# phi(K) as one maximum on VectorE, with new instruction orders, in a linear-attention and gated-GELU block on one core

## The chip, the core and the metric

The kernel runs on one NeuronCore of one Trainium2 chip. Its metric is device time in microseconds, the median of several runs. The engines are named as the profile names them: PE (TensorE), DVE (VectorE), ACT (ScalarE), POOL (GpSimd) and SP (SyncE, which here only issues DMAs).

## The reference

One sequence of 2048 tokens with 448 features goes through a pre-norm linear attention (16 heads of 28) and a gated-GELU feed-forward layer of width 1792, each with a residual. All inputs are bf16.

```python
qkv = (layernorm(x) @ wqkv)                     # split into q, k, v per head
phi = lambda t: jnp.where(t > 0, t + 1, jnp.exp(t)) + 1e-6
pq, pk = phi(q), phi(k)
kv = einsum("bhsd,bhse->bhde", pk, v)
z = einsum("bhsd->bhd", pk)
num = einsum("bhqd,bhde->bhqe", pq, kv)
den = einsum("bhqd,bhd->bhq", pq, z)[..., None] + 1e-6
h = x + merge_heads(num / den) @ wo
g, u = layernorm(h) @ w_gate, layernorm(h) @ w_up
out = h + (gelu_tanh(g) * u) @ w_down
```

## The kernel before

Tokens are cut into 16 tiles of 128 (T = 16); a pair is two tiles. The kernel is a graph of small named tasks. Each belongs to one engine, and every engine works through its tasks in an order written out as numbers in `ORDERS` (lines 15 to 49; one string each for PE, ACT, DVE, POOL and SP). The function `place` (line 129) takes those orders; the waits between engines are semaphores worked out from what each task reads and writes. So an order says only when an engine comes to a task; a task still waits for its inputs and for the buffer that it overwrites. `HOLD` (line 50) names, for some tasks that wait for two others, which of the two waits is written first.

Stage 1 (to about 34 us). For each tile: statistics (`bnst1_t`, `bnag1_t`, lines 413 and 414, DVE), the reciprocal root in two activations (`ln1_t`, `rstd1_t`, lines 420 and 422, ACT), normalisation and transpose. Tiles 0 to 3 are normalised on DVE (`normD_t`, line 435) and transposed on PE in two halves (`tr0_t`, `tr1_t`, line 443), copied out by ACT (`evxA_t`) and DVE (`evxD_t`, line 450). Tiles 4 to 15 are normalised on POOL (`normP_t`, line 453) and transposed by a DMA that SP issues (`xT_t`, line 455).

Then come the projections, four matmuls each: `k_t` and `q_t` (`proj`, line 469), in the sequence that PE's order gives. They take their PSUM banks in turn from four (`slot`), in the sequence of `SEQ`, so that each waits until the one four places earlier has been read. The contraction is over 448 rows in four chunks of 128; the last chunk has 64 rows of weights, and its other 64 rows of `wqk_sb` are set to zero (`wqkpad`, line 364). In the transposed input the rows that meet them hold ones, for the columns 448 to 511 of `xnn` are set to 1 (`ones2`, line 386).

phi(K) is made from the projected tile in PSUM, psK, in three steps: ACT writes exp(K) to `e1` (`ek_t`, line 480); DVE clamps it to at most 1 + 1e-6 (`ck_t`, line 481); DVE adds to it the larger of K and 1e-6 (`pk_t`, line 482). The sums over tokens are kept as four accumulating groups of matmuls over all 16 tiles, in PSUM banks 4 to 7: each tile gives four matmuls (line 488, `pt4_t`; from tile 10 on split as `pt1_t`, chunk 3, and `pt3_t`, chunks 0 to 2), with the normalised input `xnn` as weights and `pk` as the moving operand. The ones in `xnn` make the lower half of chunk 3 the sum z.

From the sums to the attention output (about 32 to 50 us): z is copied to both halves of `zbc` (`z1` on ACT, `z0` on DVE, lines 514 and 515), the four sums go to `pt_sb` (`evpD_3` and `evpD_2` on DVE, `evpA_0` and `evpA_1` on ACT, lines 516 to 521), `kv` multiplies them by the value weights (line 527), `kvm` (line 531) masks out other heads, `w2_c` multiplies by wo (line 547). For the first pair, `cq`, `aq`, `t1`, `dr`, `deA`, `rd` and `pn` (lines 564 to 576) make phi(Q) divided by its denominator. PE fills the waits with the projections `q_4` to `q_15`, then transposes the first pair of normalised h (`trh`, line 654).

Stage 2 (about 50 us to the end): for every chunk of tiles `gu` (lines 731 and 733) makes gate and up projections in two PSUM banks each, ACT applies the GELU (`ge`, line 751), DVE multiplies (`hm`, line 753); the down projections (`down`, lines 678 and 697), the final additions (`fo`) and the stores (`do_t`) follow. The attention outputs of later pairs (`outA`, `outB`, lines 627 and 628) are placed between them.

Of the kernel before, what the change touches and what calls it, by code (L numbers as in the profile page):

```python
# [48 lines left out]
)  # L49
HOLD = {  # L50
    66: (36,), 141: (140,), 165: (164,), 214: (213,), 216: (215,), 323: (302,), 326: (324,), 431: (340,), 704:
    (564,), 735: (734,), 781: (672,), 839: (836,), 849: (846,), 854: (852,), 866: (865,),
# [176 lines left out]
def bass_sequential_preLN__linear_attn_block__glu_gated_geglu__prompt_kernel(  # L229
# [3 lines left out]
    T, P = S // 128, S // 256  # L233
# [15 lines left out]
    with es:  # L249
        block = es.enter_context(nc.Block())  # L250

        def sb(name, shape, dt):
            return es.enter_context(nc.sbuf_tensor(name, shape, dt))
# [28 lines left out]
        pk = sb("pk", [128, PK_R, D], BF16)  # L282
# [7 lines left out]
        eps_d = sb("eps_d", [128, 1], F32)  # L290
        rd = sb("rd", [128, 4, H], F32)
# [24 lines left out]
        b_epsd = _Buf("epsd")  # L316
# [66 lines left out]
        op("pool", lambda e: e.memset(eps_d[:], EPS), [], [b_epsd], "epsd")  # L383
        op("pool", lambda e: e.memset(mhalf[:], -0.5), [], [b_mhalf], "mhalf")
# [87 lines left out]
        def proj_reads(t, b):  # L472
            return [(b_xnT[t][0], 0), (b_xnT[t][1], 2), (b[0], 0), (b[1], 3), (b_wpad[0], 3)]

        def k_tile(t):
# [4 lines left out]
            eks.append(act_exp(lambda e: e.activation(e1[:, i, :], psK, AF.Exp), [b_ps[bk]], [b_e1[i]], "ek_%d" % t))  # L480
            op("dve", lambda e: e.tensor_scalar(e1[:, i, :], e1[:, i, :], 1.0 + EPS, 0.0, ALU.min, ALU.max), [b_e1[i]], [b_e1[i]], "ck_%d" % t)
            op("dve", lambda e: e.scalar_tensor_tensor(pk[:, ip, :], psK, EPS, e1[:, i, :], ALU.max, ALU.add), [b_ps[bk], b_e1[i]], [b_pk[ip]], "pk_%d" % t)  # L482
            groups = ((3, 0, 1, 2),) if t < PT_SPLIT else ((3,), (0, 1, 2))
            for cs in groups:
                def fpt(e, cs=cs):
                    ins = None
                    for c in cs:
                        ins = e.matmul(ps[:, BK_PT[c], 0:D], xnn[:, t % XN_R, c * 128:(c + 1) * 128], pk[:, ip, :], start=(t == 0), stop=(t == T - 1))  # L488
                    return ins
                G.add("pe", fpt, r=[b_xn[t % XN_R], b_ones2, b_pk[ip]], w=[b_ps[BK_PT[c]] for c in cs], name="pt%d_%d" % (len(cs), t))  # L490
# [332 lines left out]
```

## Time and profile before

| | |
|---|---|
| Median of 3 runs | 190.51 us (190.46 to 190.75) |
| Span of the profiled execution, first to last instruction | 188.3 us |
| Its own time | not recorded apart; at the median, 2.2 us lie outside the span |
| PE busy | 184.3 us, 98% |
| DVE busy | 129.3 us, 69% |
| ACT busy | 76.5 us, 41% |
| POOL busy | 50.0 us, 27% |
| DMA moved | 17.11 MB, mean 91 GB/s |

The busy time of PE is a modelled one: matmuls overlap, and each is shown from its start to a modelled end, so that two neighbours 0.19 us apart are shown with 0.35 us each. How fast PE works is read from the distance between starts. Rows of a timeline give the start, the length, engine, line, operation, output<-input and the count of merged instructions; in square brackets stands the idle time before and what ended it.

### The profile page before, as it was taken

The page shows a single profiled execution, that of the slowest core. Times are in us where ns is not written, and L with a number is a line of the kernel's source. Part 1 is how long each engine was busy: PE and PEld are TensorE (multiplying, and loading weights), DVE is VectorE, ACT ScalarE, POOL GpSimd, SP SyncE. Part 2 cuts the span into 40 slices and gives each one's busy share as a digit, 9 for nine tenths or more (in the row PEclk, how much of TensorE's full clock was granted, in tenths as well). Part 3 has the DMA queues.
Part 4 walks back from the last instruction along what each step waited for, and adds up shares of the span by engine and source line. Part 5 has one row for each costly group of instructions (what it writes and reads, how often), then busy time and mean ns, then how long its engine had stood idle before and what let it go on. Part 6 is the DMA issues. An engine that isn't in the chain of part 4 may idle for free.

```text
span 188.3 us, 4459 instructions
## 1 busy us (share of the span) xinstructions
PE 184.3 (98%) x1813; PEld 109.2 (58%) x1813; DVE 129.3 (69%) x330; ACT 76.5 (41%) x220; POOL 50.0 (27%) x91
## 2 busy tenths in 40 slices
PE   7999999999999999999999999999999999999994
PEld 7545555555688788965554555555545545454554
DVE  4999959999899998786796762562645244335432
ACT  3878752799963231432234222321242222224100
POOL 6067910704505686033614000206100000000000
PEclk9999999999999999999999999999999999999999
DMA  5996458999393526820005720000096000002024
GB/s 169 387 231 88 96 104 194 218 222 174 65 320 64 95 52 116 84 52 0 0 3 98 144 54 0 0 3 2 3 135 111 3 0 24 3 0 98 3 79 140
DMA packets 35076, 17.11 MB, mean 91 GB/s; under 512 B 26864, under 2 KB 33648, under 8 KB 35056
## 3 DMA queue, kind: packets, MB, share of 16 engines
q1 hardware_dynamic: 34432, 16.32, 41.1%
q10 hardware_dynamic: 624, 0.52, 0.8%
q8 instruction: 14, 0.23, 0.5%
q14 instruction: 6, 0.05, 0.1%
HBM read 8.26 MB, written 1.84 MB: 54 GB/s over the span
## 4 chain that ended last, share of the span: by engine, by line
PE 94%; DVE 3%; DMA 1%; issue 0%
PE ps L733 38%; PE ps L697 19%; PE ps L469 12%; PE ps L731 9%; PE ps L488 6%; PE ps L627 3%; PE ps L678 3%; PE ps L628 2%; DMA x_sb<-in_A_x_dram 1%; DVE st L413 1%; PE ps L617 1%; PE ps L547 1%; PE ps L527 1%; PE ps L443 0%; PE ps L654 0%; DVE den L572 0%
## 5 line engine op out<-in xcount | busy, mean ns | idle before, releaser
L733 PE MATMUL ps<-hnT,wgu_sb 64*128 64x512 bf16 (+1 forms) x490 | 88.8, 333 | 0.0
L731 PE MATMUL ps<-hnT,wgu_sb 64*128 64x512 bf16 (+1 forms) x490 | 88.6, 333 | 0.0
L751 ACT ACTIVATE gl<-ps 128x256 bf16<-128x256 f32 x112 | 36.6, 383 | 85.3 <-PE ps L731 84.4
L753 DVE TENSOR_TENSOR hh<-ps,gl 128x256 bf16<-128x256 f32 x112 | 42.1, 416 | 41.4 <-ACT gl L751 41.3
L733 PEld LDWEIGHTS ps<-hnT,wgu_sb 64*128 64x128 bf16 x490 | 45.2, 94 | 32.9 <-DVE hh L753 3.4
L731 PEld LDWEIGHTS ps<-hnT,wgu_sb 64*128 64x128 bf16 x490 | 45.4, 94 | 2.5
L697 PE MATMUL ps<-wd_sb,hh 64*128 64x448 bf16 x392 | 41.5, 349 | 0.0
L697 PEld LDWEIGHTS ps<-wd_sb,hh 64*128 64x128 bf16 x392 | 23.2, 94 | 14.5
L469 PE MATMUL ps<-wqk_sb,xnT 128*128 128x448 bf16 x128 | 27.4, 353 | 0.0
L413 DVE BATCH_NORM_STATS2 st<-x_sb 128x6 f32<-128x448 bf16 x32 | 19.2, 612 | 1.8 <-DMA x_sb<-in_A_x_dram 1.7
L585 POOL TENSOR_TENSOR t<-pq,zbc 128x448 f32<-128x448 bf16 x12 | 12.3, 1042 | 23.7 <-DVE pq L583 22.0
L469 PEld LDWEIGHTS ps<-wqk_sb,xnT 128*128 128x128 bf16 x128 | 11.9, 98 | 11.4 <-DVE pk L482 0.8
L488 PE MATMUL ps<-pk,xnn 128*128 128x448 bf16 x64 | 13.9, 352 | 0.0
L627 PE MATMUL ps<-w,pqnT 64*128 64x448 bf16 x49 | 11.5, 349 | 0.1
L425 POOL TENSOR_SCALAR ln<-mv 128x2 f32<-128x2 f32 x7 | 2.0, 291 | 35.2 <-DVE mv L414 35.0
L480 ACT ACTIVATE e<-ps 128x448 bf16<-128x448 f32 x16 | 8.5, 539 | 5.6 <-PE ps L469 5.5
L628 PE MATMUL ps<-pt_sb,pqnT 64*128 64x448 bf16 x42 | 10.2, 350 | 0.0
L633 DVE TENSOR_TENSOR x_sb<-ps,x_sb 128x448 bf16<-128x448 f32 x16 | 9.6, 616 | 0.7 <-PE ps L628 0.6
L662 POOL TENSOR_SCALAR hn<-x_sb,nm,rs 128x448 bf16<-128x448 bf16 x14 | 9.9, 719 | 0.4
L482 DVE SCALAR_TENSOR_TENSOR pk<-ps,e 128x448 bf16<-128x448 f32 x16 | 9.8, 617 | 0.1
L488 PEld LDWEIGHTS ps<-pk,xnn 128*128 128x128 bf16 x64 | 6.3, 98 | 5.9 <-DVE pk L482 0.3
L453 POOL TENSOR_SCALAR xnn<-x_sb,nm,rs 128x448 bf16<-128x448 bf16 x12 | 8.9, 744 | 2.2 <-ACT rs L422 1.9
(85 smaller groups left out, 160.5 us busy)
## 6 DMA issues: line engine op xcount, KB each, us to landing
out_dram<-x_sb SPq DMA_DIRECT2D x15, 112.0 KB, 1.8
wd_sb<-in_B_w_down_dram SPq DMA_DIRECT2D x1, 1568.0 KB, 8.4
x_sb<-in_A_x_dram SPq DMA_DIRECT2D x3, 448.0 KB, 5.9
wgu_sb<-in_B_w_gate_dram SPq DMA_DIRECT2D x1, 896.0 KB, 12.1
wgu_sb<-in_B_w_up_dram SPq DMA_DIRECT2D x1, 896.0 KB, 16.5
wgu_sb<-in_B_w_gate_dram SPq DMA_DIRECT2D x1, 672.0 KB, 6.1
wgu_sb<-in_B_w_up_dram SPq DMA_DIRECT2D x1, 672.0 KB, 8.5
wo_sb<-in_A_wo_dram SPq DMA_DIRECT2D x1, 392.0 KB, 7.5
```

What stands on the lines that cost most here:

```text
L413: op("dve", lambda e: e.bn_stats(st[:, t, :], src_ap), [b_src], [b_st[t]], "bnst%s_%d" % (tag, t))
L469: ins = e.matmul(ps[:, bk, 0:D], xnT[:, t, k, :], wqk_sb[:, k, c0:c0 + D], start=(k == 0), stop=(k == 3))
L488: ins = e.matmul(ps[:, BK_PT[c], 0:D], xnn[:, t % XN_R, c * 128:(c + 1) * 128], pk[:, ip, :], start=(t == 0), stop=(t == T - 1))
L585: op("pool", lambda e, n=n: e.tensor_tensor(t1[:, n, :], pq[:, a + n, :], zbc[:, :], ALU.mult), [b_pq[a + n]] + b_z, [b_t1[n]], "t1p_%d" % ...
L627: e.matmul(ps[:, BK_OUT[0], 0:D], pqnT[ra, i2, sg // 2, :], w2[ra, sg // 2, :], start=(sg == 0), stop=(sg == 5))
L628: ins = e.matmul(ps[:, BK_OUT[1], 0:D], pqnT[rb, i2, 3 + (sg + 1) // 2, :], (w2 if sg == 6 else w2s)[rb, sg // 2, :], start=(sg == 0), sto ...
L662: op("pool", lambda e, t=t, sh=sh: e.tensor_scalar(hn[:, sh, 0:D], x_sb[:, t, :], nm2[:, t:t + 1], rs2[:, t:t + 1], ALU.add, ALU.mult), [b ...
L697: ins = e.matmul(ps[:, bko[half][n], 0:D], hh[rows, j, sl[n]], wd_sb[rows, j, :], start=(j == 0 and (half == 0 or p == 6)), stop=(j == NJ ...
L731: first = e.matmul(psG[:, jj * N:(jj + 1) * N], wgu_sb[A_, k, j * 128:(j + 1) * 128], hnT[A_, ka_, c0:c0 + N], start=(k == 0), stop=(k == ...
L733: ins = e.matmul(psU[:, jj * N:(jj + 1) * N], wgu_sb[B_, k, j * 128:(j + 1) * 128], hnT[B_, kb_, c0:c0 + N], start=(k == 0), stop=(k == NK ...
L751: G.add("act", lambda e, gi=gi, cs_=cs_, psG=psG: e.activation(gl[:, gi, cs_], psG[:, cs_], AF.Gelu_apprx_tanh), r=[b_ps[BK_G[i]]], w=[b_g ...
L753: op("dve", lambda e, dst=dst, srcU=srcU, srcL=srcL: e.tensor_tensor(dst, srcU, srcL, ALU.mult), [b_ps[BK_U[i]], b_glh], [b_ar[j_][t % HR] ...
```

## The change

In `k_tile` one of two DVE instructions per tile is dropped. The projection now yields K + 1 in PSUM: the upper half of the weights' last chunk gets a row of ones for K (`w1row`), which meets the ones in the transposed input. The exponential subtracts that one again by a bias of -1. phi(K) without its 1e-6 is then max(min(exp(K), 1), K + 1), one scalar_tensor_tensor. The missing 1e-6 is made up in the sums: `pk` becomes two columns wider (450), these are set to 1e-6, and the sums over tokens run over 449 columns, so that column 448 of each sum is what 1e-6 in every entry would have added; it is added as a value per partition when the sums leave PSUM. For the two sums that ACT copies, DVE first copies that column to `ecol` in SBUF; for z the constant 2048 x 1e-6 (`eps_s`) is the bias.

All five orders are new, and `HOLD` now names one wait for nearly every task (over 600 entries). In the excerpt the orders and `HOLD` are left out.

```diff
-        pk = sb("pk", [128, PK_R, D], BF16)
+        pk = sb("pk", [128, PK_R, D + 2], BF16)
...
+        op("dve", lambda e: e.memset(wqk_sb[64:65, 3, D:2 * D], 1.0), [b_wpad[0]], [b_w1r], "w1row")
...
+        op("pool", lambda e: e.memset(neg1[:], -1.0), [], [b_neg1], "neg1")
+        op("pool", lambda e: e.memset(eps_s[:], S * EPS), [], [b_epss], "epss")
+        op("pool", lambda e: e.memset(pk[:, :, D:D + 2], EPS), [], [b_pke], "pkeps")
...
-            eks.append(act_exp(lambda e: e.activation(e1[:, i, :], psK, AF.Exp), [b_ps[bk]], [b_e1[i]], "ek_%d" % t))
-            op("dve", lambda e: e.tensor_scalar(e1[:, i, :], e1[:, i, :], 1.0 + EPS, 0.0, ALU.min, ALU.max), [b_e1[i]], [b_e1[i]], "ck_%d" % t)
-            op("dve", lambda e: e.scalar_tensor_tensor(pk[:, ip, :], psK, EPS, e1[:, i, :], ALU.max, ALU.add), [b_ps[bk], b_e1[i]], [b_pk[ip]], "pk_%d" % t)
+            eks.append(act_exp(lambda e: e.activation(e1[:, i, :], psK, AF.Exp, bias=neg1[:, 0:1]), [b_ps[bk], b_neg1], [b_e1[i]], "ek_%d" % t))
+            op("dve", lambda e: e.scalar_tensor_tensor(pk[:, ip, 0:D], e1[:, i, :], 1.0, psK, ALU.min, ALU.max), [b_ps[bk], b_e1[i]], [b_pk[ip]], "pk_%d" % t)
...
-                        ins = e.matmul(ps[:, BK_PT[c], 0:D], xnn[:, t % XN_R, c * 128:(c + 1) * 128], pk[:, ip, :], start=(t == 0), stop=(t == T - 1))
+                        ins = e.matmul(ps[:, BK_PT[c], 0:D + 1], xnn[:, t % XN_R, c * 128:(c + 1) * 128], pk[:, ip, 0:D + 1], start=(t == 0), stop=(t == T - 1))
...
-        op("act", lambda e: e.activation(zbc[B_, :], ps[B_, BK_PT[3], 0:D], AF.Identity), [b_ps[BK_PT[3]]], [b_z[1]], "z1")
+        op("dve", lambda e: e.tensor_copy(ecol[:, 0:2], ps[:, BK_PT[0]:BK_PT[0] + 2, D]), [b_ps[BK_PT[0]], b_ps[BK_PT[1]]], [b_ecol], "ecol")
+        op("act", lambda e: e.activation(zbc[B_, :], ps[B_, BK_PT[3], 0:D], AF.Identity, bias=eps_s[B_, 0:1]), [b_ps[BK_PT[3]], b_epss], [b_z[1]], "z1")
...
-        op("dve", lambda e: e.tensor_copy(pt_sb[A_, 3, :], ps[A_, BK_PT[3], 0:D]), [b_ps[BK_PT[3]]], [b_pt[3]], "evpD_3")
+        op("dve", lambda e: e.tensor_scalar(pt_sb[A_, 3, :], ps[A_, BK_PT[3], 0:D], ps[A_, BK_PT[3], D:D + 1], None, ALU.add), [b_ps[BK_PT[3]]], [b_pt[3]], "evpD_3")
...
-                op("act", lambda e, c=c: e.activation(pt_sb[:, c, :], ps[:, BK_PT[c], 0:D], AF.Identity), [b_ps[BK_PT[c]]], [b_pt[c]], "evpA_%d" % c)
+                op("act", lambda e, c=c: e.activation(pt_sb[:, c, :], ps[:, BK_PT[c], 0:D], AF.Identity, bias=ecol[:, c:c + 1]), [b_ps[BK_PT[c]], b_ecol], [b_pt[c]], "evpA_%d" % c)
```

(`evpD_2` changes as `evpD_3` does.) Read as names of tasks, the orders differ at these places. PE, start: `tr0_0 tr1_0 tr1_1 tr0_1 k_0 tr1_2 tr0_2 k_1 tr0_3 k_2 tr1_3 q_0 k_3`. DVE, start: `wqkpad w1row wvpad bnst1_0 bnst1_1 bnag1_0 bnag1_1 bnst1_2 normD_0 bnag1_2 normD_1 bnst1_3 evxD_0`; before it was `wvpad wqkpad bnst1_0 bnag1_0 bnst1_1 bnag1_1 normD_0 bnst1_2 normD_1 bnag1_2 bnst1_3 evxD_0`. PE, K tiles: `k_4 pt4_3 q_3 k_5 k_7 k_6` for `k_4 pt4_3 k_5 q_3 k_6 pt4_4 k_8 pt4_5 k_7`; SP issues `xT_7` before `xT_8`, not after it. PE, end of the sums: `pt1_15 pt3_12 pt3_13 pt3_14 pt3_15 q_4 q_5 kv` for `pt1_15 pt3_13 pt3_14 pt3_15 q_5 q_4 kv`. DVE there: `evpD_3 z0 t1d_0 dr_0 ecol evpD_2 dr_1 aq_3 dr_2 rd_0 pn_0 kvm` for `evpD_3 z0 aq_1 t1d_0 dr_0 evpD_2 rd_0 dr_1 dr_2 kvm`. PE, end: `downA_6 downB_6`, then the first half of tile 15, tile 14, the second half of tile 15; before it was tile 14 and both halves of tile 15. In the gated stage (`gu`, `ge`, `hm`) many neighbours change places.

More of the change, by code (lines that the diff above doesn't have):

```diff
@@ L15 @@
 ORDERS = (
[33 rows of a table removed]
[33 rows of a table added]
 )
 HOLD = {
-    66: (36,), 141: (140,), 165: (164,), 214: (213,), 216: (215,), 323: (302,), 326: (324,), 431: (340,), 704:
-    (564,), 735: (734,), 781: (672,), 839: (836,), 849: (846,), 854: (852,), 866: (865,),
[78 rows of a table added]
 }
@@ L290, in bass_sequential_preLN__linear_attn_block__glu_gated_geglu__prompt_kernel @@
         eps_d = sb("eps_d", [128, 1], F32)
+        neg1 = sb("neg1", [128, 1], F32)
+        eps_s = sb("eps_s", [128, 1], F32)
+        ecol = sb("ecol", [128, 2], F32)
         rd = sb("rd", [128, 4, H], F32)
@@ L315, in bass_sequential_preLN__linear_attn_block__glu_gated_geglu__prompt_kernel @@
             _Buf(n) for n in ("ident", "ones", "mones", "mtmp", "mask", "eps", "mhalf", "powtmp"))
-        b_epsd = _Buf("epsd")
+        b_epsd, b_epss, b_ecol, b_neg1, b_pke, b_w1r = _Buf("epsd"), _Buf("epss"), _Buf("ecol"), _Buf("neg1"), _Buf("pke"), _Buf("w1r")
         b_st1, b_mv1, b_nm1, b_ln1, b_rs1 = bufs("st1", T), bufs("mv1", T), bufs("nm1", T), bufs("ln1", T), bufs("rs1", T)
@@ L472, in proj_reads @@
         def proj_reads(t, b):
-            return [(b_xnT[t][0], 0), (b_xnT[t][1], 2), (b[0], 0), (b[1], 3), (b_wpad[0], 3)]
+            return [(b_xnT[t][0], 0), (b_xnT[t][1], 2), (b[0], 0), (b[1], 3), (b_wpad[0], 3)] + ([(b_w1r, 3)] if b is b_wk else [])
         def k_tile(t):
@@ L487, in fpt @@
                     for c in cs:
-                        ins = e.matmul(ps[:, BK_PT[c], 0:D], xnn[:, t % XN_R, c * 128:(c + 1) * 128], pk[:, ip, :], start=(t == 0), stop=(t == T - 1))
+                        ins = e.matmul(ps[:, BK_PT[c], 0:D + 1], xnn[:, t % XN_R, c * 128:(c + 1) * 128], pk[:, ip, 0:D + 1], start=(t == 0), stop=(t == T - 1))
                     return ins
-                G.add("pe", fpt, r=[b_xn[t % XN_R], b_ones2, b_pk[ip]], w=[b_ps[BK_PT[c]] for c in cs], name="pt%d_%d" % (len(cs), t))
+                G.add("pe", fpt, r=[b_xn[t % XN_R], b_ones2, b_pke, b_pk[ip]], w=[b_ps[BK_PT[c]] for c in cs], name="pt%d_%d" % (len(cs), t))
         def q_tile(t):
@@ L511, in bass_sequential_preLN__linear_attn_block__glu_gated_geglu__prompt_kernel @@
             dma("sp", wgu_sb[B_, :, cs], B_w_up[:, cs].rearrange("(k p) n -> p k n", p=64), [b_wu[i]], "dwu%d" % i, after=xts[-1:])
-        op("act", lambda e: e.activation(zbc[B_, :], ps[B_, BK_PT[3], 0:D], AF.Identity), [b_ps[BK_PT[3]]], [b_z[1]], "z1")
+        op("dve", lambda e: e.tensor_copy(ecol[:, 0:2], ps[:, BK_PT[0]:BK_PT[0] + 2, D]), [b_ps[BK_PT[0]], b_ps[BK_PT[1]]], [b_ecol], "ecol")
+        op("act", lambda e: e.activation(zbc[B_, :], ps[B_, BK_PT[3], 0:D], AF.Identity, bias=eps_s[B_, 0:1]), [b_ps[BK_PT[3]], b_epss], [b_z[1]], "z1")
         op("dve", lambda e: e.tensor_copy(zbc[A_, :], zbc[B_, :]), [b_z[1]], [b_z[0]], "z0")
-        op("dve", lambda e: e.tensor_copy(pt_sb[A_, 3, :], ps[A_, BK_PT[3], 0:D]), [b_ps[BK_PT[3]]], [b_pt[3]], "evpD_3")
+        op("dve", lambda e: e.tensor_scalar(pt_sb[A_, 3, :], ps[A_, BK_PT[3], 0:D], ps[A_, BK_PT[3], D:D + 1], None, ALU.add), [b_ps[BK_PT[3]]], [b_pt[3]], "evpD_3")
         for c in range(3):
             if c in (0, 1):
-                op("act", lambda e, c=c: e.activation(pt_sb[:, c, :], ps[:, BK_PT[c], 0:D], AF.Identity), [b_ps[BK_PT[c]]], [b_pt[c]], "evpA_%d" % c)
+                op("act", lambda e, c=c: e.activation(pt_sb[:, c, :], ps[:, BK_PT[c], 0:D], AF.Identity, bias=ecol[:, c:c + 1]), [b_ps[BK_PT[c]], b_ecol], [b_pt[c]], "evpA_%d" % c)
             else:
-                op("dve", lambda e, c=c: e.tensor_copy(pt_sb[:, c, :], ps[:, BK_PT[c], 0:D]), [b_ps[BK_PT[c]]], [b_pt[c]], "evpD_%d" % c)
+                op("dve", lambda e, c=c: e.tensor_scalar(pt_sb[:, c, :], ps[:, BK_PT[c], 0:D], ps[:, BK_PT[c], D:D + 1], None, ALU.add), [b_ps[BK_PT[c]]], [b_pt[c]], "evpD_%d" % c)
         def fkv(e):
```

144 rows, old and new, of tables (HOLD, ORDERS) are left out of this document.

## The prediction

> **What bounds the kernel now.** I read the page's summary and chain first, then the busy time by stage, then the costliest groups of the step that is edited, and last the single instructions at the few places where TensorE is not back to back.
>
> ```profile
> span 188.3 us, 4459 instructions
> ...
> PE 184.3 (98%) x1813; PEld 109.2 (58%) x1813; DVE 129.3 (69%) x330; ACT 76.5 (41%) x220; POOL 50.0 (27%) x91
> ...
> PE 94%; DVE 3%; DMA 1%; issue 0%
> ```
>
> TensorE (PE) is busy for 184.3 of 188.3 us, and 94% of the chain that ended last is its work. Busy time alone could hide slow matmuls, so the stages come next: PE is the first pair of numbers in each row, VectorE (DVE) the third.
>
> ```profile
> 6.30:34.23 27.93, 27.92 (x157) 14.12 (x154) 25.20 (x75) 18.40 (x56) 11.98 (x29) 1.00 0.74 172
> 34.23:50.14 15.91, 15.79 (x117) 8.77 (x116) 15.36 (x36) 15.28 (x39) 6.26 (x6) 1.00 0.91 173
> 50.14:174.76 124.62, 124.62 (x1403) 74.42 (x1401) 80.39 (x200) 39.30 (x119) 28.94 (x46) 1.00 0.30 57
> ```
>
> From 6.30 to 174.76 us PE idles 0.13 us, at the full granted clock (1.00). The first row is the stage that the change edits: DVE is busy for 25.20 of 27.93 us there, but it keeps PE waiting for 0.01 us. So time saved on DVE is not on the path. What can move the end is: the first 6 us, the waits in the second row, a new wait inside the full stages, and the tail.
>
> **The step that is edited.** Two DVE instructions per K tile make phi(K): the clamp (line 481) and the sum (line 482).
>
> ```profile
> L482 DVE SCALAR_TENSOR_TENSOR pk<-ps,e 128x448 bf16<-128x448 f32 x16 | 9.8, 617 | 0.1
> ...
> L481 DVE TENSOR_SCALAR e<-e 128x448 bf16<-128x448 bf16 x16 | 4.2, 271 | 2.3 <-ACT e L480 2.2
> ```
>
> The clamp goes: 16 x 0.271 = 4.3 us less on DVE. The instruction that stays has the same form (one bf16 operand in SBUF, one f32 operand in PSUM, bf16 out), so I keep 0.617 us for it. The path from a K tile to its phi becomes one step shorter, but in this stage PE takes other tiles meanwhile. Worth on the path: 0, hidden by PE's own 27.92 us. The bias operand of the exponential gets no price; the activation reads one value per partition more. The row of ones in the weights (one DVE memset of one partition) and the three small GpSimd memsets are issued before the first input lands; DVE idles 1.73 us there (first row of the next fence).
>
> **The start.** Every delay here moves the whole PE stream. The new DVE order takes the statistics of tile 1 before it finishes those of tile 0, and the statistics of tile 2 before it normalises tile 0.
>
> ```profile
> 3.34 0.63 DVE L413 BATCH_NORM_STATS2 st<-x_sb 128x6 f32<-128x448 bf16 x1 [1.73 <-DMA x_sb<-in_A_x_dram]
> 4.00 0.18 DVE L414 BATCH_NORM_AGGREGATE mv<-st 128x2 f32<-128x6 f32 x1
> 4.10 0.59 DVE L413 BATCH_NORM_STATS2 st<-x_sb 128x6 f32<-128x448 bf16 x1
> 4.73 0.18 DVE L414 BATCH_NORM_AGGREGATE mv<-st 128x2 f32<-128x6 f32 x1
> 4.83 0.36 DVE L435 TENSOR_SCALAR xnn<-x_sb,mv,rs 128x448 bf16<-128x448 bf16 x1
> 5.11 0.62 DVE L413 BATCH_NORM_STATS2 st<-x_sb 128x6 f32<-128x448 bf16 x1
> 5.65 0.38 DVE L435 TENSOR_SCALAR xnn<-x_sb,mv,rs 128x448 bf16<-128x448 bf16 x1
> ```
> ```profile
> 6.09 0.40 PE L443 MATMUL ps<-ident,xnn 128*128 128x128 bf16 x4 [0.39 <-DVE xnn L435]
> ```
> ```profile
> 0.79 0.87 SPq L346 DMA_DIRECT2D x_sb<-in_A_x_dram  x2
> ```
> ```profile
> x_sb<-in_A_x_dram SPq DMA_DIRECT2D x1, 224.0 KB, 3.4
> ```
>
> Now: an independent instruction follows a statistics instruction after 0.54 us (5.11 to 5.65). After: statistics of tile 0 at 3.34 as before, of tile 1 at 3.88, the two aggregates at about 4.4 and 4.5. Tiles 2 and 3 are the second of the two issues that start at 0.79, so issued at about 1.2, and they land 3.4 later, at 4.6; their first statistics run 4.63 to 5.25. The normalisation of tile 0 then starts at 5.2 instead of 4.83. That of tile 1 needs its own reciprocal root from ScalarE (ACT). From an aggregate's end to the normalisation that uses it are 0.65 us (4.18 to 4.83); tile 1's aggregate ends at 4.7, and its logarithm queues behind tile 0's two activations for about 0.35 us, which gives 5.65 to 5.7, as now. PE's second transposes (6.09) wait for exactly that, so tile 0's 0.4 us are lost inside the old 0.39 us of idle. The DVE copy that the first projection needs comes one aggregate (some 0.1 us) earlier in the new order. I take -0.05 us; ends: -0.1, and +0.4 if tile 0's delay goes through in full.
>
> **The extra column.** The 64 matmuls of line 488 go from 448 to 449 columns. Twenty of them take 3.78 us (next fence, 30.45 to 34.23), 0.189 each; in proportion that is 0.4 ns each, +0.03 us in all. No row has an odd width. The upper end is a rival below.
>
> **From the K sums to the kv matmuls.** This is the one wait in mid-kernel.
>
> ```profile
> 32.73 0.62 DVE L516 CAST pt_sb<-ps 64x448 bf16<-64x448 f32 x1
> 33.37 0.39 DVE L515 COPY zbc<-zbc 64x448 f32<-64x448 f32 x1
> 33.79 0.39 DVE L565 TENSOR_TENSOR pq<-pq,eq 128x448 bf16<-128x448 bf16 x1
> 34.10 0.62 DVE L569 TENSOR_TENSOR t<-pq,zbc 128x448 f32<-128x448 bf16 x1
> 34.76 0.62 DVE L572 TENSOR_REDUCE den<-t 128x16 f32<-128x448 f32 x1
> 35.29 0.61 DVE L521 CAST pt_sb<-ps 128x448 bf16<-128x448 f32 x1
> ```
> ```profile
> 30.45 3.95 PE L488 MATMUL ps<-pk,xnn 128*128 128x448 bf16 x20
> 34.23 1.68 PE L469 MATMUL ps<-wqk_sb,xnT 128*128 128x448 bf16 x8
> 35.96 1.03 PE L527 MATMUL ps<-pt_sb,wv_sb 128*112 128x112 bf16 x16
> ```
> ```profile
> 34.43 0.98 ACT L519 ACTIVATE pt_sb<-ps 128x448 bf16<-128x448 f32 x2 [1.16 <-PE ps L488]
> ```
>
> Now: the eight projection matmuls at 34.23 last 8 x 0.189 = 1.51, so PE is ready at 35.74 and waits 0.22 us for the DVE chain, whose last copy ends at 35.90. After: the group pt1_15, which starts that chain, stands ahead of 12 matmuls instead of 9, so 3 x 0.189 = 0.57 us earlier, and the chain begins at 32.16. It runs evpD_3 (0.62), z0 (0.39), t1d_0 (0.62), dr_0 (0.62), with some 0.03 us at each step, and is through at about 34.5; aq_1 (0.39) has left it. There comes the new wait: ecol, a copy of two columns from PSUM, can start when the last K sum is written, at 34.43 (where ACT starts now); both ACT copies wait for it, and behind them in ACT's queue wait deA_0 and the exponentials of q tiles 5 and 4, and on PE the kv matmuls. The price of ecol is not in the trace. The smallest DVE rows quoted are 0.18 us (two results a partition); a full copy from PSUM is 0.61. I take 0.18, since it reads two columns: ecol 34.5 to 34.65, ACT 34.7 to 35.65, DVE's evpD_2 inside the same time, kv possible at 35.7, PE ready at 35.74: -0.22 us. With 0.61 it would be 36.1, +0.15. The chain behind it (kvm, w2) gets dr_1, aq_3, dr_2, rd_0 and pn_0 ahead of kvm on DVE; in these durations kvm is done about 0.2 us before PE, which has q_7 and q_8 first, asks for it. Cover: those two tiles, 1.51 us.
>
> **The transposed inputs.** In the new order k_7 takes the place that k_6 has now, third of the tiles at 16.23 below, and its input xT_7 is the fourth transpose of the SyncE (SP) queue; now it is the fifth.
>
> ```profile
> 10.31 6.30 SPq L455 DMA_TRANSPOSE xnT<-xnn  x4
> ```
> ```profile
> L455 SPq DMA_TRANSPOSE xnT<-xnn x12: 1189/1264/1656, 10.3 to 26.0; - x12
> ...
> DMA to landing us min/median/max: 2.5/2.7/4.1
> ```
> ```profile
> 16.23 2.27 PE ps L469 x12
> ```
> ```profile
> q8 instruction: 14, 0.23, 0.5%
> ```
>
> The third tile of that row starts at 16.23 + 2 x 0.76 = 17.7 in the chain's times, which are ends, so it asks for its input at about 17.6. The first four transposes take 6.30 us to issue, though four of 1.264 are 5.06: SP waited 1.2 us for normalised tiles. With the shorter DVE queue I expect it not to wait: fourth issue at 10.31 + 3 x 1.3 = 14.2, landing 2.7 later, at 16.9, 0.7 us early. With the longest landing, 4.1, it would be 18.3, 0.7 late; with SP's old wait and 2.7, 18.1, 0.5 late. I take 0, the median row; ends 0 and +0.7.
>
> Fourteen DMA packets of instructions (0.23 MB, 16 KB each) share the DMA engines with these transposes, and one falling onto a transpose could make the long landing. The Trainium skill, Runtime: NRT & Kernel Launch, section Instruction fetch mechanics, says that engines refill their instructions in 16 KiB blocks over a DMA queue of their own and that crossing a block is mostly hidden; by that rule the term is 0, by the longest landing +0.7. No row quoted here shows which holds.
>
> **The gated stage and the tail.** From 50.14 on, all orders are new, but PE has nothing to give there; I take 0, with a loss up to 0.4 as the other end (about the size of one late DVE instruction of 0.4 to 0.6 us). At the end the two halves of tile 15 stand around tile 14, so that three stores instead of one are issued in the last 1.3 us.
>
> ```profile
> out_dram<-x_sb SPq DMA_DIRECT2D x15, 112.0 KB, 1.8
> ...
> out_dram<-x_sb SPq DMA_DIRECT2D x2, 56.0 KB, 1.6
> ```
>
> The last store (56 KB) may land like one in a row of stores, 1.8, instead of 1.6: 0 to +0.2, I take +0.1. PE's own order costs nothing there: the same 42 matmuls.
>
> **Sum.** -0.05 + 0.03 - 0.22 + 0 + 0 + 0.1 = -0.14 us against the span of 188.3. The runs' median is 190.51, so 2.2 us lie outside the span, and the change leaves them: 190.37, say 190.4. A measurement of this kernel can tell about 0.2%, 0.38 us, from no change; this is inside.
>
> **Rivals.** (A) Slower: xT_7 lands late. For: 4.1 us is in the trace, SP waited 1.2 us among the first four, and the new order brings k_7 forward. Against: the median landing leaves 0.7 us. It makes the kernel slower by over 0.38 us once it lands after 17.6 + 0.14 + 0.38 = 18.1; price 0.5 to 0.7, time 190.9 to 191.1. (B) Slower: one late DVE instruction in the gated stage, 0.4 to 0.6 us: 190.8 to 191.0; against it, PE idles 0.00 us there under the present order. (C) Slower: the 449th column is paid as a block of 64: 64 x 0.189 x 64/448 = 1.7 us, 192.1; the rows neither show nor exclude it. The Trainium skill, TensorE: Matmul & The Clock Gate, section Wait — 56ns, not 53.3ns?, gives N columns at 2.4 GHz plus some 2.5 ns, without blocks; the 0.189 us at 448 agree, and by it the term stays 0.03. (D) Faster: the start gains too. All of the 0.39 us of idle at 6.09 and the 0.22 us at kv are 0.6 us: 189.9 without the tail's loss. For: DVE is the releaser of both. Against: tile 1's normalisation comes out at the same 5.65.
>
> **Chances.** Forecast 0.49; A 0.22, B 0.08, C 0.03; D 0.18. Faster 0.18, same 0.49, slower 0.33. The forecast's own bounds are 190.15 to 190.85. The range 190.0 to 191.1 takes in A and most of B and the upper half of D; left out are C, the low half of D, and a little of B: about 0.16.
>
> **What would show it.** In the profile after: line 481's group gone and line 482's at 0.617 us; DVE's busy time down by some 4 us with the span about the same; the second transposes at 6.1; pt matmuls 0.189 to 0.190 apart; kv starting 8 x 0.189 after the projections ahead of it, with no DVE wait; k_7 without idle. I am wrong if PE idles before k_7 or within the gated stage by more than 0.4 us, if line 488's pace changes, or if the first projections start more than 0.2 us off 6.3.

## The result, and the profile after

The changed kernel takes 192.63 us (median of 4 runs, 192.25 to 193.73) where the kernel before takes 190.56 beside it: 1.0117 times as long, 95% interval 1.0085 to 1.0148. It is slower by 2.1 us, outside the predicted range. The profiled execution took 192.72 us.

The page after, its first lines and the chain of work that ended last:

```profile
span 190.7 us, 4454 instructions
...
PE 185.0 (97%) x1813; PEld 115.3 (60%) x1813; DVE 128.0 (67%) x316; ACT 77.9 (41%) x220; POOL 51.9 (27%) x94
...
PE 78%; DMA 9%; DVE 6%; SPq 3%; issue 1%; POOL 0%; ACT 0%
```

PE's share of the chain fell from 94% to 78%, and DMA's rose from 1% to 9%. PE itself works as long as before (185.0 us against 184.3). So what the kernel lost is waiting, most of it for DMAs. The busy time by stage, cut at the same pieces of work as in the prediction (window, its length, then PE's busy time):

```profile
6.30:35.53 29.23, 28.54 (x157) 14.02 (x156) 22.39 (x59) 20.16 (x56) 12.64 (x31) 1.00 0.76 171
35.53:51.44 15.91, 15.85 (x116) 8.52 (x116) 15.30 (x37) 15.30 (x39) 5.88 (x6) 1.00 0.82 159
51.44:177.44 126.00, 124.97 (x1402) 81.66 (x1400) 81.22 (x199) 38.66 (x117) 30.59 (x46) 1.00 0.27 61
```

The first stage is 29.23 us long instead of 27.93, the middle is the same, and the last is 126.00 instead of 124.62 (the last cut does not fall quite alike: from the first gate or up matmul to the start of the last one it is 125.79 instead of 124.61). The granted clock is 1.00 throughout. Who PE waited for (total, times, longest; matmuls overlap, so the work itself is put back somewhat more than the idle time shown):

```profile
PE ps L814 <- DMA hnT<-hn: 0.6, 1, 0.6
PE ps L552 <- DMA xnT<-xnn: 0.4, 1, 0.4
PE ps L526 <- DVE xnn L518: 0.4, 1, 0.4
PE ps L710 <- DMA pqnT<-pqn: 0.4, 1, 0.4
PE ps L552 <- DVE xnT L533: 0.2, 1, 0.2
```

(Left out is the first row, in both kernels a wait of 1.0 to 1.1 us before the warm-up matmuls.) Before, only the wait of 0.4 for DVE's xnn was there. Three DMA transposes are new in the list, one of each kind; measured from one start of a matmul to the next, over PE's usual pace, they cost 0.61 us (k_7 on xT_7), 0.57 (outA_3 on oT_3) and 0.83 (gu4_42 on hT_13), 2.0 us of the 2.4 by which the span grew. At the start, k_0 begins at 6.66 instead of 6.32, but its second half no longer waits 0.18 for a DVE copy, so that PE is 0.15 behind there; k_3 then waits 0.33. The differences that are left are small and go both ways.

Grouped by form, the instructions that the new arithmetic touched (busy time, mean ns):

```profile
L563 ACT ACTIVATE e<-ps,neg 128x448 bf16<-128x448 f32 x16 | 10.0, 631 | 4.5 <-PE ps L552 4.1
L564 DVE SCALAR_TENSOR_TENSOR pk<-e,ps 128x448 bf16<-128x448 bf16 x16 | 9.5, 611 | 5.6 <-ACT e L563 5.6
L602 ACT ACTIVATE pt_sb<-ps,ecol 128x448 bf16<-128x448 f32 x2 | 1.2, 630 | 1.9 <-DVE ecol L596 1.9
L599 DVE TENSOR_SCALAR pt_sb<-ps 64x448 bf16<-64x448 f32 x1 | 0.7, 681 | 0.4 <-PE ps L570 0.4
```

The instruction that stays on DVE keeps its duration (611 ns, 617 before), but the exponential takes 631 ns where line 480 had 539, the two sums on ACT 630 where they had 540, and the one on DVE that is shown 681 where it had 617.

### The profile page after: what moved, and what is told of

Its sections match the earlier page's. It is cut to its first block, busy times and chain, and to the rows that moved or that the text cites. A ratio compares the mean times of both kernels' runs of the same rounds, so it can differ in the third digit from the quotient of the medians.

```text
span 190.7 us, 4454 instructions
## 1 busy us (share of the span) xinstructions
PE 185.0 (97%) x1813; PEld 115.3 (60%) x1813; DVE 128.0 (67%) x316; ACT 77.9 (41%) x220; POOL 51.9 (27%) x94
## 4 chain that ended last, share of the span: by engine, by line
PE 78%; DMA 9%; DVE 6%; SPq 3%; issue 1%; POOL 0%; ACT 0%
PE ps L814 32%; PE ps L780 18%; PE ps L552 9%; PE ps L570 5%; PE ps L816 4%; DMA x_sb<-in_A_x_dram 3%; PE ps L761 3%; PE ps L710 3%; DMA pqnT<-pqn 2%; DVE st L496 2%; DMA hnT<-hn 2%; SPq L748 2%; PE ps L711 2%; DMA xnT<-xnn 1%; DVE hh L836 1%
## 5 line engine op out<-in xcount | busy, mean ns | idle before, releaser
L836 DVE TENSOR_TENSOR hh<-ps,gl 128x256 bf16<-128x256 f32 x112 | 42.6, 415 | 42.6 <-ACT gl L834 42.6
L814 PEld LDWEIGHTS ps<-hnT,wgu_sb 64*128 64x128 bf16 x490 | 46.0, 94 | 27.2 <-DMA hnT<-hn 1.1
L816 PEld LDWEIGHTS ps<-hnT,wgu_sb 64*128 64x128 bf16 x490 | 45.8, 94 | 2.1 <-DVE hh L836 0.2
L780 PE MATMUL ps<-wd_sb,hh 64*128 64x448 bf16 x392 | 39.5, 349 | 0.0
L668 POOL TENSOR_TENSOR t<-pq,zbc 128x448 f32<-128x448 bf16 x12 | 14.0, 1178 | 19.4 <-DVE pq L666 15.7
L500 POOL TENSOR_SCALAR nm<-mv 128x1 f32<-128x1 f32 (+1 forms) x19 | 4.5, 240 | 40.4 <-DVE mv L497 40.0
L570 PE MATMUL ps<-pk,xnn 128*128 128x449 bf16 x64 | 13.7, 353 | 0.0
L564 DVE SCALAR_TENSOR_TENSOR pk<-e,ps 128x448 bf16<-128x448 bf16 x16 | 9.5, 611 | 5.6 <-ACT e L563 5.6
L563 ACT ACTIVATE e<-ps,neg 128x448 bf16<-128x448 f32 x16 | 10.0, 631 | 4.5 <-PE ps L552 4.1
```

Of the source, the lines that this page charges most:

```text
L570: ins = e.matmul(ps[:, BK_PT[c], 0:D + 1], xnn[:, t % XN_R, c * 128:(c + 1) * 128], pk[:, ip, 0:D + 1], start=(t == 0), stop=(t == T - 1))
L668: op("pool", lambda e, n=n: e.tensor_tensor(t1[:, n, :], pq[:, a + n, :], zbc[:, :], ALU.mult), [b_pq[a + n]] + b_z, [b_t1[n]], "t1p_%d" % ...
L780: ins = e.matmul(ps[:, bko[half][n], 0:D], hh[rows, j, sl[n]], wd_sb[rows, j, :], start=(j == 0 and (half == 0 or p == 6)), stop=(j == NJ ...
L814: first = e.matmul(psG[:, jj * N:(jj + 1) * N], wgu_sb[A_, k, j * 128:(j + 1) * 128], hnT[A_, ka_, c0:c0 + N], start=(k == 0), stop=(k == ...
L816: ins = e.matmul(psU[:, jj * N:(jj + 1) * N], wgu_sb[B_, k, j * 128:(j + 1) * 128], hnT[B_, kb_, c0:c0 + N], start=(k == 0), stop=(k == NK ...
L836: op("dve", lambda e, dst=dst, srcU=srcU, srcL=srcL: e.tensor_tensor(dst, srcU, srcL, ALU.mult), [b_ps[BK_U[i]], b_glh], [b_ar[j_][t % HR] ...
```

## What was tried

The theories in the expectations: **O**, the new orders put the transposes too close to their uses; **F**, the arithmetic itself costs the time; **I**, fetches of instructions collide with transposes. `HOLD` always goes with the orders that it belongs to, so no run tells the two apart. Lines of these kernels are numbered differently from the changed kernel's, since the orders are written with other line breaks. Ratios are to the kernel before, run on the same chip.

### One half of the change at a time

```diff
 # e1: kernel after, with ORDERS and HOLD of before
-  DVE: ... ck_0 ... ck_15 ...
+  DVE: ... wqkpad w1row ...   evpD_3 z0 aq_1 ecol t1d_0 dr_0 evpD_2 ...
+  POOL: ... epsd neg1 pkeps ...  mhalf epss ...
 # e2: kernel before, with ORDERS and HOLD of after
+  DVE: ... ck_t pk_t ...   (the clamp directly ahead of each sum)
```

> The new arithmetic in the orders and held waits of the kernel before: the 16 clamps are left out of VectorE's order, the six new small steps are put in beside their neighbours, nothing else moves. Theory O (the orders lose the time: three transposes by DMA, xT_7, oT_3 and hT_13, now land 0.61, 0.57 and 0.83 us after PE asks for them): 190.2 to 190.8, and none of these three waits on PE. Theory F (the arithmetic loses it: the exponential with a bias operand takes 631 ns against 539, the evictions with one 634 against 544): 191.6 to 192.6. Theory I (fetches of PE's program, one DMA packet of 16 KB each, collide with the transposes by chance): about 190.5, with one landing more or less late.

> The old arithmetic in the new orders and held waits, each clamp put directly ahead of its addition on VectorE. Theory O: 192.0 to 193.5, with the waits for oT_3 and hT_13 there as in the changed kernel, since these stages hold no clamp. Theory F: 190.3 to 191.0. Theory I: anywhere from 190.5 to 193, by where the fetches fall.

The orders alone: 193.07 us, 1.0125 (1.0105 to 1.0144), the whole loss and a little more, but not all at the same places. In the trace of e2 PE waits 0.63 for oT_3 and 0.29 for hT_13 (per start of matmul; the gated stage is 125.30 us long from its first matmul to the start of its last, 124.61 before), and not for xT_7. Its first stage loses more than that of the changed kernel: PE leaves it at 36.43 us (35.53 in the changed kernel, 34.23 before), after waiting some 1.5 us in seven places for pk. With the clamps back, DVE does not keep up with the new orders there. So in the first stage the new orders need the shorter arithmetic, and e2 does not price them by themselves.

The arithmetic alone: 191.93, 1.0059 (1.0043 to 1.0075), more than O said and within what F said. The list of PE's waits of e1 tells why:

```profile
PE ps L547 <- DVE pt_sb L541: 1.2, 1, 1.2
PE ps L427 <- POOL eps_d L400: 1.0, 1, 1.0
PE ps L489 <- DMA xnT<-xnn: 0.9, 1, 0.9
```

The second row is the warm-up at the very start, in every kernel. The third is k_4, whose input xT_4 landed at 15.77, 5.1 us after its issue and beside a fetch of 16 KB of instructions at 12.84. The first is `kv` waiting for evpD_2, which I had let stand behind ecol, t1d_0 and dr_0: my placing, not the arithmetic. So F was not settled yet.

### Better places for the new copy

```diff
 # DVE's order around the end of the sums, formula and other orders as in e1
-  evpD_3 z0 aq_1 ecol t1d_0 dr_0 evpD_2 rd_0 dr_1 dr_2 kvm rd_2 kvd   # e1
+  evpD_3 z0 t1d_0 ecol evpD_2 aq_1 dr_0 rd_0 dr_1 dr_2 kvm rd_2 kvd   # e5
+  evpD_3 z0 t1d_0 ecol evpD_2 aq_1 dr_0 rd_0 dr_1 kvm kvd dr_2 rd_2   # e8 (and ACT: eq_5 rq_5 eq_4)
+  evpD_3 z0 aq_1 t1d_0 ecol evpD_2 dr_0 rd_0 dr_1 dr_2 kvm rd_2 kvd   # e11
 # e12: e11, and evxD_3 ahead of pk_0
```

> The new arithmetic in the old orders once more, now with the copy of the sums (ecol) and evpD_2 ahead of aq_1 and dr_0 on VectorE. In the first such run kv waited 1.25 us for evpD_2, which ended at 38.50, because ecol stood ahead of t1d_0 and both it and dr_0 stood ahead of evpD_2: that was the placing, not the arithmetic. Theory O (arithmetic about free): 190.3 to 190.9, the wait before kv at 0.1 or less. Theory F (arithmetic costs 1 us or more): 191.4 to 192.0. Theory I: the fetch near 12.8 us stays and holds up xT_4 in some executions, for up to 1.0 us, so single times up to 191.6.

> The new arithmetic in the old orders as in the last such run (191.29, 0.53 over the kernel before), with the masked copies kvm and kvd put directly behind dr_1 on VectorE instead of behind dr_2, and rq_5 ahead of eq_4 on ScalarE. In that run kv ended at 37.49 and kvm began at 38.79, behind dr_2, which waited for POOL's t1p_2 until 38.25; w2_2 waited for kvm until 39.46, and q_8 0.23 for rq_5. Theory O (the rest of the 0.53 is these small waits of the order, not the arithmetic): 190.6 to 191.0. Theory F (the arithmetic keeps at least 0.5): 191.2 to 191.4.

> The new arithmetic in the old orders, third placing: aq_1 and t1d_0 where the kernel before has them, ecol and evpD_2 behind them and ahead of dr_0. In the two earlier placings aq_1 stood behind evpD_2, so that POOL's t1p_1 began 1.75 us after z0's end (36.18 against 34.43) where the kernel before has 0.51, and the whole row of denominators with it; kvm or pn_1 then came late, and PE waited before w2_2 or tro_1. Theory O (the arithmetic itself is free, what was left came from my placing): t1p_1 within 0.6 of z0, no wait above 0.25 us between kv and trh_0, 190.5 to 190.9. Theory F (the arithmetic costs 0.3 or more by its longer exponentials and evictions): 191.1 to 191.4.

> The same with one step more: evxD_3 ahead of pk_0 on VectorE. In three of the four runs of this kind k_3 waited 0.27 to 0.36 us for evxD_3, which stood behind pk_0, whenever the load dx4 landed at 8.4 or later (8.05 in the one without the wait, 7.89 in the kernel before). Theory O: k_3 no longer waits; up to 0.3 us under the run beside it, 190.3 to 190.8. If that wait is covered by a later one (xT_4): the same time as the run beside it within 0.2 us.

| | time, us | ratio (95%) |
|---|---|---|
| e5 | 191.29 | 1.0033 (1.0017 to 1.0049) |
| e8 | 192.09 | 1.0082 (1.0069 to 1.0095) |
| e11 | 190.78 | 1.0016 (1.0002 to 1.0029) |
| e12 | 190.98 | 1.0023 (1.0012 to 1.0035) |

e5 lies between what O and F said. e8 missed: it took away the wait before w2_2 and made a larger one behind it.

```profile
40.23 0.35 PE L567 MATMUL ps<-wo_sb,hh 112*128 112x448 bf16 x1
42.06 0.62 PE L619 MATMUL ps<-ident,pqn 128*128 128x128 bf16 x8 [1.48 <-ACT w L571]
```

With kvm and kvd early, dr_2 and dr_3 came later on DVE, so deA_3 came later on ACT, and ACT's copies of w2, queued behind it, too (41.04 with PE out of the sums at 34.33; in e5 40.81 and 34.84). e11 is the best of these places, and the timeline of POOL in e5, then in e11, shows what was wrong in e5:

```profile
36.18 3.03 POOL L589 TENSOR_TENSOR t<-pq,zbc 128x448 f32<-128x448 bf16 x3 [10.09 <-DVE pq L585]
```
```profile
34.40 1.35 POOL L589 TENSOR_TENSOR t<-pq,zbc 128x448 f32<-128x448 bf16 x1 [8.85 <-DVE pq L585]
```

DVE's aq_1 (0.39 us) releases POOL's row of products. Behind evpD_2 it let them begin 1.8 us later, and all denominators with them. In e11 the first stage and the gated one are back to the length of before (28.00 and 124.62 against 27.93 and 124.62); the middle is 16.20 instead of 15.91:

```profile
span 188.6 us, 4449 instructions
...
PE 184.0 (98%) x1813; PEld 108.6 (58%) x1813; DVE 126.6 (67%) x316; ACT 77.7 (41%) x220; POOL 49.7 (26%) x94
...
PE 94%; DVE 3%; DMA 1%; issue 0%
```
```profile
6.30:34.30 28.00, 27.98 (x156) 14.35 (x154) 22.13 (x59) 19.55 (x56) 11.61 (x30) 1.00 0.74 171
34.30:50.50 16.20, 15.90 (x116) 8.65 (x116) 15.38 (x38) 15.43 (x39) 6.29 (x6) 1.00 0.91 170
50.50:175.12 124.62, 124.62 (x1401) 74.33 (x1399) 80.37 (x200) 39.29 (x119) 28.87 (x46) 1.00 0.28 57
```

So the arithmetic alone costs 0.16% (0.02 to 0.29), some 0.3 us, and F accounts for a seventh of the loss. e12 was no gain: in its trace k_3 waits 0.32 us for pk_0, now behind evxD_3, while in that of e11, where the load came early enough, it waits for neither.

### Which half of the orders

```diff
 # every task up to pair 0 (trh_0, trh_1) keeps the place of one kernel,
 # every task from pair 1 on that of the other; new arithmetic in both
+  e9:  orders of after up to pair 0, orders of before from pair 1
+  e10: orders of before (as in e5) up to pair 0, orders of after from pair 1
```

> The new arithmetic with the change's orders and held waits for all work up to pair 0 of the second half (its transposes trh_0 and trh_1), and the old orders for all that follows. Along PE the changed kernel's profile is 1.30 us behind the kernel before at gu2_0 and 2.48 behind at its last matmul. Theory O: the first stage's share, 191.8 to 192.2, with the wait for xT_7 and none for oT_3 or hT_13 above 0.2 us. Theory I (lateness is taken up or handed on by where a fetch falls): 191.2 to 192.6, with another transpose late in the second half.

> The counterpart: the old orders up to pair 0 (with the placing that gave 191.29) and the change's orders for all that follows. Theory O: the second half's share of 1.2 us on top of 191.29, 192.2 to 192.6, with waits on PE for oT_3 and hT_13. Theory I: 191.3 to 192.6 by where the fetches near 60 and 147 us fall against these transposes; if one of them is clear, the wait there goes.

e9: 193.61 us, 1.0185 (1.0154 to 1.0216). e10: 193.82, 1.0171 (1.0147 to 1.0195). Both are over 1 us above what either theory said. e9's time says little on the start: at the seam between the two orders PE waited 1.3 us for DVE's hn, which neither kernel does. Ahead of the seam, PE leaves the sums at 34.88 us (35.53 in the changed kernel, 34.23 before), with 0.2 before k_7 in place of 0.61, so the same orders lost half as much there in this trace. How much of the first stage's 1.3 us belongs to the orders, and how much to one execution, stays open. Behind the seam it is clean: from the first gate or up matmul to the start of the last are 124.61 us (53.02 to 177.64), as in the kernel before, so the old orders run it at full pace behind the new start too. e10, with the new orders in the gated stage and the old start, has the waits again (and one of 1.0 us per start of matmul, on hT_10, that the changed kernel does not have):

```profile
PE ps L1193 <- DMA hnT<-hn: 1.6, 2, 0.8
...
PE ps L1089 <- DMA pqnT<-pqn: 0.4, 1, 0.4
```

This settles that the gated stage's loss is made by its own orders. Cut in the same way, the stage is 124.61 to 124.62 us long in all eight traces with the old orders in it (before, e1, e5, e6, e8, e9, e11, e12), and 125.30 to 127.00 in the six with the new ones (the changed kernel, e2, e3, e4, e7, e10), whatever the arithmetic. The two halves do not add up to the whole (e10 alone loses more than after). Why is not shown: in e10's trace PE came to the stage later than in the changed kernel (52.24 and 51.44), and this was the slowest of its five executions (194.72).

### Why the transposes land late

Take oT_3, a transpose into the tile pqnT. The first line is its time from issue to landing in the changed kernel, the second the same in before, e3, e7 and e11:

```profile
DMA to landing us min/median/max: 4.5/4.5/4.5
```
```profile
DMA to landing us min/median/max: 2.9/2.9/2.9
```

A transpose is done when 16 reports have come, which I take for one from each DMA engine. In the changed kernel 15 come between 60.71 and 60.87, and the last at 62.46. The DMA queues between 60.41 and 61.45:

```profile
q8 instruction: 1, 0.02, 6.1%
q1 hardware_dynamic: 2, 0.00, 0.3%
```

6.1% of 16 engines for 1.04 us is one engine for 1.02 us: a packet of 16 KB of instructions, from 60.42 to 61.43. There are 14 such packets for 1813 matmuls, 78 to 164 matmuls apart, so I take them for PE's program. The two packets of the transposes' own queue in that time are 4 bytes each and were moved at 61.42 and 61.43, behind the fetch: the report that the transpose is complete. The last data had been moved by 60.42. One fetch, served in between, cost 1.6 us: 1.0 until these two packets were moved, and 0.6 because the report then came 1.03 us after them, where the other 15 came some 0.5 behind such packets. Why the last one took longer is not shown.

The landing of oT_3 follows the start of that fetch by 2.04 us in the changed kernel, 2.06 in e2, 2.06 in e4 and 2.06 in e10. Where the fetch came after the last of these small packets, by 0.03 us in e7 and 0.28 in before, nothing happened; nor did it in e1 and e11, where the fetch began 0.05 and 0.06 before the last of them, perhaps on another DMA engine than theirs. Over all fourteen traces, 152 of the transposes issued after 52 us met no fetch (8 or 16 KB) between issue and landing, and the slowest of these took 3.19 us; of the 114 that met one, 62 took longer, up to 5.18. So in these traces no transpose lands late without a fetch, but not every fetch makes one late. To move it alone:

```diff
-  for _ in range(WARM):                       # 40 matmuls of 128 columns
-      ins = e.matmul(ps[:, 3, 0:128], ones_bf[:], ones_bf[:], ...)
+  for i in range(24):                         # 16 of 256 and 8 of 128
+      n = 2 if i < 16 else 1
+      ins = e.matmul(ps[:, 3, 0:n * 128], ones_bf[:], ones_bf[:] n times, ...)
```

> The changed kernel with its 40 warm-up matmuls of 128 columns made into 16 of 256 and 8 of 128: the same columns, 16 matmuls fewer ahead of everything, so that PE crosses each boundary of its program 16 matmuls later (the fetches at 14.3 and 60.4 us should come near 17 and 62). Theory I: xT_7 lands near 16.9 and oT_3 near 60.9, both waits of PE (0.61 and 0.57) go, 191.3 to 191.8; the wait for hT_13 stays, as the fetch beside it is another engine's. Theories O and F: 192.4 to 192.8, the waits where they were.

> The kernel before, nothing of the change in it, with 16 matmuls fewer in the warm-up and the same columns, so that its program is fetched 16 matmuls later. Theory I: the fetch at 15.2 us comes at 18 to 19 and that at 59.0 at 60 to 61; the transposes beside them land 0.8 to 1.7 us late, and PE waits for the ones it needs at once: 190.9 to 192.3. If only the orders matter and the kernel before has slack for such lateness: 190.4 to 190.7.

e3: 192.91 us, 1.0117 (1.0101 to 1.0134). Theory I was right on both waits and wrong on the sum. The fetch came at 61.97, oT_3 took 2.9 us, and neither it nor xT_7 (landing at 17.05) held PE up. In their place PE waited for two later xT, beside which three fetches now fell (18.50, 18.94 and 19.03), with 5.8 us to landing for one of them, and still for hT_13:

```profile
PE ps L1096 <- DMA xnT<-xnn: 1.2, 2, 0.7
...
PE ps L1358 <- DMA hnT<-hn: 0.9, 1, 0.9
```

e6, the same edit in the kernel before: 190.79, 1.0003 (0.9987 to 1.0018). With the old orders this move makes no difference, though in its trace transposes took up to 5.5 us to land. So fetches hit transposes in every kernel (in before, several take 4.5 to 5.1 us and PE does not wait); the new orders are those that have too little slack for it.

For xT_7 the fetch (14.33 to 15.54) worked one step earlier, on the issue. SP's four issues in the changed kernel, then the first five of e3:

```profile
L538 SPq DMA_TRANSPOSE xnT<-xnn x4: 1188/1279/2300, 11.0 to 16.0; - x4
```
```profile
L1082 SPq DMA_TRANSPOSE xnT<-xnn x5: 1189/1265/1292, 10.5 to 15.8; - x5
```

The issue of xT_6 took 2.30 us instead of 1.27, and xT_7 was issued at 16.00; it then landed after an ordinary 2.5. In all fourteen traces 37 of 462 transposes took over 1.5 us to issue, and each of them overlapped a fetch.

For hT_13 the order counts more. SP's queue before PE's wait, and three lines of DVE's timeline:

```profile
139.27 3.22 SPq L748 DMA_TRANSPOSE hnT<-hn  x2
142.53 0.58 SPq L791 DMA_DIRECT2D out_dram<-x_sb  x1
143.16 2.57 SPq L748 DMA_TRANSPOSE hnT<-hn  x2
```
```profile
129.09 0.61 DVE L716 TENSOR_TENSOR x_sb<-ps,x_sb 128x448 bf16<-128x448 f32 x1
...
134.31 0.76 DVE L836 TENSOR_TENSOR hh<-ps,gl 128x256 bf16<-128x256 f32 x2 [4.27 <-ACT gl L834]
134.98 0.62 DVE L496 BATCH_NORM_STATS2 st<-x_sb 128x6 f32<-128x448 bf16 x1
```

The source of hT_13 was normalised by 126.1, but DVE's wrap_13, which completes it, stands at 138.80, and SP takes hT_15, hT_14, do_5 and hT_12 first; hT_15 and hT_14 wait for tile 14, whose residual (129.09) stands behind products of the gated stage and whose statistics (134.98) stand behind one more, which came after 4.27 us of idle time. DVE had time; its order did not use it. hT_13 was issued at 144.42; a fetch of 8 KB at 146.94 then put one engine's report 0.86 us behind the others.

### Mending the orders

```diff
 # e4, on the changed kernel
-  PE: k_5 k_7 k_6          gu2_5 outA_3 gu2_6 outB_3 downA_0
+  PE: k_5 k_6 k_7          gu2_5 gu2_6 outA_3 downA_0 outB_3
-  DVE: ... hm1_35 wrap_12 ... wrap_14 wrap_13     SP: oT_7 do_7 do_2 hT_15 hT_14 do_5 hT_12 hT_13
+  DVE: ... bnag2_15 wrap_12 wrap_13 ...           SP: oT_7 hT_12 hT_13 do_7 do_2 hT_15 hT_14 do_5
 # e7: the same without the outA_3 line; DVE's start as in before; PE k_10 k_9 pt4_7 k_11
```

> The changed kernel with three repairs of its orders: k_6 ahead of k_7 on PE; outA_3 behind gu2_6 and outB_3 behind downA_0; wrap_12 and wrap_13 on VectorE right behind bnag2_15, and hT_12 and hT_13 right behind oT_7 on SP. Theory O: the three waits of 0.61 + 0.57 + 0.83 = 2.0 us go, 190.6 to 191.0, what is left over the kernel before being the later start. Theory I: the same time, but the landings of xT_7 and oT_3 stay late by the fetches (18.5 and 62.5), only nobody waits for them. Theory F: 192.2 to 192.7.

> The changed kernel with its orders mended in the start and late: VectorE's first ten normalization steps in the order of before (bnag1_0 ahead of bnst1_1, normD_0 ahead of bnst1_2), k_6 ahead of k_7 and k_9 ahead of k_11 on PE, wrap_12 and wrap_13 right behind bnag2_15, hT_12 and hT_13 right behind oT_7; outA_3 stays where the change has it. Theory O: the start comes 0.3 to 0.4 earlier, the waits for xT_7, xT_11 and hT_13 go, that for oT_3 (0.57) stays or grows by what PE is earlier: 190.9 to 191.6. Theory I: part of the time gained in the start is taken again by the next late transpose, 191.3 to 192.2.

e4: 193.22 us, 1.0124 (1.0092 to 1.0156), 2.2 us above what O said. All three waits are gone, and PE waits elsewhere:

```profile
PE ps L1095 <- DMA xnT<-xnn: 1.1, 1, 1.1
...
PE ps L1359 <- DVE hh L1379: 1.0, 2, 0.7
```

Coming earlier, PE now stands before xT_11, and twice before a product of DVE: once (0.43 per start of matmul), as outA_3 no longer lies ahead of gu2_6, because DVE has the product behind cqP_5 and a copy, and once (0.87, at 78.38) because it stands behind wrap_7 and aqP_7. e7, which also has ek_9 ahead of ek_10 on ACT: 192.01, 1.0072 (1.0047 to 1.0096), within what I had said of it under I: the waits for xT_7 and hT_13 stay away, oT_3 is not hit, and PE stands idle 0.87 us before hT_10 instead, beside a fetch at 112.30. Neither version is faster than the kernel before.

## Why the prediction was wrong, by its own steps

**The gated stage: this step failed.** I took 0, with a loss of up to 0.4 for "one late DVE instruction". PE waited 1.40 there (0.57 + 0.83), and the stage is 1.2 longer. I asked only whether DVE could be late there, and not whether the transposes that feed it could (19 of the 21 are issued after 50 us), though I had quoted the landing times (2.7 as the median, 4.1 the longest) for xT_7. The stage showed no idle time because the old orders leave room: oT_3 landed 1.5 us before outA_3 asked (59.18 and 60.64). The new orders leave about 1.1 (an ordinary landing at 60.86, asked for at 61.94), and then a fetch takes 1.6. In the kernel before, this fetch came 0.28 us too late to meet oT_3, and that is luck of the old orders: their 1.5 would not quite have covered it. "Many neighbours change places" was in front of me; each change of place spends such room, and I priced none.

**The transposed inputs: rival A came true, at its price** (0.61 against 0.5 to 0.7), in part by luck, for the cause was another than the long landing that it was priced by. The fourth issue was at 16.00, not 14.2: 0.65 from the later first issue (10.96 against 10.31), 1.03 from the stretched issue of xT_6, little from waiting for normalised tiles. Of the 1.2 us that I read as SP's waiting in the kernel before, 0.4 was such an issue too (1.66 us, beside a fetch at 15.21). That a fetch could do this was in the prediction, priced by landing; it acts on the issue too. The Trainium skill, Runtime: NRT & Kernel Launch, section Instruction fetch mechanics, has the fetch mostly hidden. For the engine that fetches, the trace agrees (before, PE idles 0.13 us in all beside 13 such fetches); for a transfer beside it, the changed kernel shows 1.0 us on an issue and 1.6 on a landing.

**The start: wrong in sign.** I took -0.05, with +0.4 as the other end; k_0 came 0.34 later, of which 0.15 is left when it is through. Tile 0's delay did go through: both halves of the transposes waited together for 0.41 us at 5.81. Tiles 2 and 3 also landed at 4.81 instead of 4.61, which is not the change's. Nor is the 0.33 before k_3 shown to be: over the runs dx4, the next load, landed anywhere from 7.89 to 8.69 (8.69 in the changed kernel), and in e1, e5 and e10, where it landed at 8.36 or later, k_3 waits 0.27 to 0.36 with the old start as well.

**From the sums to kv: mis-sized.** Predicted -0.22, measured -0.09 (the wait fell from 0.22 to 0.13). ecol took 0.15, as estimated (0.18), and began at 35.77, as predicted (34.5, and by then everything is 1.3 later). What was wrong is that a bias operand "gets no price": it costs 92 ns for each exponential (631 - 539) and 90 for each sum on ACT, and the two sums, one behind the other, took 1.16 us instead of 0.98. The Trainium skill, ScalarE: Activation LUTs, section What ACT_TABLE_LOAD costs, gives some 93 ns for each operand of one value per partition; the trace agrees. Without the new orders (e11) this wait is 0.40, that is +0.18, and with 0.13 more before the first transposes that follow w2 it makes up the 0.29 by which e11's middle stage is longer, and so the 0.3 us that the arithmetic costs.

**The extra column: right.** The median step of line 570 is 190 ns instead of 189; all 64 together cost 0.08 us. Rival C (1.7 us) is excluded.

**The clamp: right on the path, mis-sized on DVE.** In e11 DVE is busy 126.6 us, 2.7 less than before and not 4.3. In the first stage it is 22.13 instead of 25.20, 0.19 for each of the 16 clamps that took 271 ns: instructions overlap their neighbours there, by 0.08 us in the rows of the prediction (4.00 + 0.18 and 4.10). The new steps on DVE take back some of it.

**The tail: no matter.** Predicted +0.1, measured 0.0: from the last matmul's end to that of the span are 2.40 us, 2.39 before.

## What to carry to other kernels

A stage in which PE never idles is not one in which nothing can be late. When an order is rewritten, look at each transfer that its consumer needs at once: how long before the use does it land now, and what does the slowest landing in the trace do to that? When a wait is taken away, PE comes earlier to the next one, so read the profile again before counting the gain (e4's trace is without 2.0 us of waits, and its time gained nothing). To judge an edit of the arithmetic, try it in the old order first; here the arithmetic is level within 0.3 us in the old orders, and the orders that came with it cost most of the 2 us.

## What I had not expected of the hardware

- The fetch of PE's program, one packet of 16 KB and about 1.0 us on one of 16 DMA engines, can be served between a transpose's data and the report of its completion. The transpose then lands 1.6 us late, though its data were there. It met oT_3 in four kernels at the same place of the program. What decides between report and fetch, 0.03 us apart in e7, stays open. No transpose after 52 us took over 3.19 us to land without a fetch beside it.
- Beside such a fetch SP's issue of a transpose took 2.30 us instead of 1.27.
- A bias of one value per partition costs an activation 92 ns, and a DVE copy from PSUM with such an operand took 681 ns instead of 617.
- In e1 t1d_0, which began 0.18 us after a product on POOL, took 1.34 us on DVE instead of 0.62; in the changed kernel it began 0.04 before one and took 0.62. Whether POOL is the cause is not shown.
